# Two-dimensional Fourier mixing and a maxout layer on one core: TensorE's order written out, the input turned on GpSimd

## Chip, cores and metric

The kernel runs on one core of one Trainium2 chip. The metric is device time in microseconds (us) of one execution. Five engines work side by side, each through its own queue in order: TensorE (PE; matmuls, with weight loads shown as PEld), VectorE (DVE), ScalarE (ACT), GpSimd (POOL) and SyncE (SP). Here GpSimd also issues the loads and SyncE the stores.

## The reference

```python
batch, seq, dim = (8, 3072, 256)
def _attn_ref(x):
    X = np.fft.fft(x, axis=1)
    X = np.fft.fft(X, axis=2)
    return X.real.astype(np.float32)

def _moe_ref(x, w1, w2, w3, w_out):          # w1..w3: 256x768, w_out: 768x256
    h = np.maximum(np.maximum(x @ w1, x @ w2), x @ w3)
    return (h @ w_out).astype(np.float32)

def reference(x, moe_w1, moe_w2, moe_w3, moe_w_out):
    a = _attn_ref(x)
    return _moe_ref(a.reshape(8 * 3072, 256), moe_w1, moe_w2, moe_w3, moe_w_out)
```

## The kernel before

**Algebra.** The transform along the sequence is split as 3072 = 24 x 128 into two stages. The transform along the model dimension is folded into the weights: gE, gO and gD are products of the cosine and sine matrices md with the differences w2-w1 and w3-w1; gw and gwr carry w1 and w_out. Because max(a, b, c) = a + max(b - a, c - a, 0), the first layer computes two differences, takes the larger and cuts it at zero; the part of w1 goes straight to the output through gw. The output rows k and 3072-k share their cosine part and differ in the sign of the sine part, so each pair of "plus" and "minus" columns comes out of one accumulation: matmuls with gE and gO give plus, and adding one with gD turns the same accumulator into minus.

**One batch.** `load_x0` (L97) has GpSimd issue 16 DMAs, which cast to bf16 and leave the input as 96 partitions x (128 sequence positions x 64 model columns). `fnet` (L264) does the sequence stages. Stage 1: 64 matmuls of 96 columns (L270), weights x0r[:, :, d], so 128 numbers with a step of 64; groups of five (`DLS`) go to one bank ps1 and are copied to ub by ScalarE (L272). VectorE folds ub into zE and zO (`fold`, L280, and small copies L289 to L297); stage 2 multiplies these with tables cos_t, sin_t, nsin_t (L318 to L326) into ps2, copied to tE and tO by ScalarE (L329); three one-column matmuls make t_mid, the middle row. GpSimd copies tE and tO in reverse to tEr and tOr (L339, L340).

**The layers.** A batch has three blocks of 512 columns and each block six units, one for each 128 columns of the hidden dimension. `unit_plus` (L343) does four 512-column matmuls into two accumulators pse2 and pse3 (L349, L350); `unit_out` (L360) evicts them: ScalarE applies relu to pse2 (L363), VectorE takes the maximum with pse3 (L364) into hp. Later `finish` adds the minus matmuls (L357), and a second `unit_out` writes hm. So a minus matmul waits for the eviction of the plus result. `l2_block` (L376) is a generator of the second layer: four times 16 matmuls of 256 columns (L367, L369, L372) into po, a copy to ot by VectorE (L392), and stores on SyncE's queue. `l2_some(11)` takes eleven of its matmuls after each unit. `l2_mid` (L402) does the middle row of all batches near the end, six rounds of its own.

**What sets the order.** GpSimd's instructions from L133 on stand under `manual_schedule`: they keep the order of the source. TensorE, ScalarE and VectorE are ordered by a planner, which looks for the next ready instruction with estimated times and mostly prefers earlier source. In the source, fnet of batch b+1 stands wholly behind the units of batch b; the planner is free to pull it forward. Buffers: two banks each for ps_f (stages 1 and 2, weight preparation), pse2, pse3 and po; two of x0, tE, tO, tEr, tOr, hp, hm; one of ub, zE and zO.

**The beginning.** Between the first four and the other twelve loads of batch 0, GpSimd makes kidx and dvec (L128, L130); VectorE computes from them the arguments of the tables (L176 to L205), ScalarE the sines. `prep_first` (L220) makes gE, gO, gD after fnet(0); `prep_second` (L240) makes gw and gwr. Loads of the weights (L139, L142) and of batch 1 follow batch 0's on GpSimd's queue.

Of the kernel before, what the change touches and what calls it, by code (L numbers as in the profile page):

```python
# [9 lines left out]
FP32 = mybir.dt.float32  # L10
# [24 lines left out]
def kernel(  # L35
# [48 lines left out]
    v2_bf = consts.tile([128, 2 * DFF], BF16, tag="v2_bf")  # L84
    v3_bf = consts.tile([128, 2 * DFF], BF16, tag="v3_bf")
# [11 lines left out]
    def load_x0(b, between):  # L97
        x0 = x0_pool.tile([96, 128 * 64], BF16, name="x0", tag="x0")
        xr = x[b].rearrange("(a bb) (g dl) -> g a bb dl", bb=128, g=4)
        x0v = x0.rearrange("p (bb dl) -> p bb dl", dl=64)  # L100
        for ch in range(4):
            if ch in between:
                between[ch]()
            for g in range(4):
                nc.gpsimd.dma_start(  # L105
                    out=x0v[g * 24:(g + 1) * 24, ch * 32:(ch + 1) * 32, :],
                    in_=xr[g, :, ch * 32:(ch + 1) * 32, :])
        return x0
# [17 lines left out]
    def between():  # L126

        nc.gpsimd.iota(kidx, [[1, 13], [24, 128]], base=0, channel_multiplier=0,  # L128
                       allow_small_or_imprecise_dtypes=True)
# [3 lines left out]
    with tc.manual_schedule(engines={mybir.EngineType.Pool}):  # L133
        x0_tiles = {0: load_x0(0, {1: between})}

# [8 lines left out]
        x0_tiles[1] = load_x0(1, {})  # L144
# [28 lines left out]
    for (dst, shift) in ((cos_t, 768.0), (sin_t, 0.0)):  # L173
        v = gen.tile([128, 13 * 128], FP32, name="v", tag="v", bufs=2)
        q = gen.tile([128, 13 * 128], FP32, name="q", tag="q", bufs=2)
# [14 lines left out]
    for fc in range(2):  # L190
# [10 lines left out]
        vi = gen.tile([128, 256], INT32, name="vi", tag="vi", bufs=2)  # L201
# [18 lines left out]
    def prep_first():  # L220

        for jh in range(2):
            cs = slice(jh * 384, (jh + 1) * 384)
            for i, (wv, vv) in enumerate(((w2_bf, v2_bf), (w3_bf, v3_bf))):
                w3d, v3d, w13d = (t.rearrange("p (fc j) -> p fc j", fc=2)[:, :, cs]
                                  for t in (wv, vv, w1_bf))
                tc.keep_in_program_order(
                    nc.vector.tensor_tensor(out=v3d, in0=w3d, in1=w13d, op=ALU.subtract))
# [8 lines left out]
                nc.vector.tensor_scalar(out=gD[i][:, cs], in0=gO[i][:, cs], scalar1=dif,  # L237
                                        scalar2=None, op0=ALU.mult)

    def prep_second():  # L240

        for jp in range(NJC // 2):
# [8 lines left out]
            nc.scalar.copy(out=g1t[:, jp * 512:(jp + 1) * 512], in_=pst)  # L251
        psw = ps_f.tile([128, 512], FP32, name="psw", tag="ps")
        for half in range(2):
            for jc in range(NJC):
# [7 lines left out]
                                op0=ALU.mult)  # L262

    def fnet(b, x0):  # L264
        x0r = x0.rearrange("p (bb dl) -> p bb dl", dl=64)
        ub = u_pool.tile([128, 64 * 96], BF16, name="ub", tag="ub")
        for (d0, d1) in DLS:
            ps1 = ps_f.tile([128, 512], FP32, name="ps1", tag="ps")
            for i in range(d1 - d0):
                nc.tensor.matmul(ps1[:, i * 96:(i + 1) * 96], x0r[:, :, d0 + i], m24blk,  # L270
                                 start=True, stop=True)
            nc.scalar.copy(out=ub[:, d0 * 96:d1 * 96], in_=ps1[:, 0:(d1 - d0) * 96])  # L272

# [9 lines left out]
        for ranges in (((20, 45),), ((10, 20), (45, 55)), ((1, 10), (55, 64))):  # L283
            for (dst, op) in ((e, ALU.add), (o, ALU.subtract)):
                for (lo, hi) in ranges:
                    for g in range(2):
                        fold(dst, op, lo, hi, g)
                if ranges[0][0] == 1:
                    nc.vector.tensor_tensor(out=dst[:, 0, 1, 0:24], in0=u[:, 0, 1, :],  # L289
                                            in1=u[:, 0, 3, :], op=op)  # L290
                    if dst is e:
                        nc.vector.tensor_copy(e[:, 0, 0, :], u[:, 0, 0, :])

        nc.vector.tensor_scalar(out=o[:, 0, 0, 1:12], in0=u[:, 0, 2, 13:24], scalar1=-1.0,
                                scalar2=None, op0=ALU.mult)
        nc.vector.tensor_copy(o[:, 0, 0, 13:24], u[:, 0, 2, 1:12])
        nc.vector.tensor_copy(o[:, 0, 0, 24:26], u[:, 0, 2, 0:13:12])  # L297
# [9 lines left out]
        for (tile_i, dst) in ((0, tE), (1, tO)):  # L307
            for g in range(3):
# [20 lines left out]
                nc.scalar.copy(out=dst[:, g * 512:(g + 1) * 512], in_=ps2)  # L329

# [10 lines left out]
        return (tE, tO), (tEr, tOr)  # L341

    def unit_plus(te, to, jc, n):  # L343

        js = slice(jc * 128, (jc + 1) * 128)
        pse2 = ps_l1.tile([128, TOKB], FP32, name="pse2", tag="pse2")
        pse3 = ps_l1.tile([128, TOKB], FP32, name="pse3", tag="pse3")
        for (pse, i) in ((pse2, 0), (pse3, 1)):
            nc.tensor.matmul(pse[:, 0:n], gE[i][:, js], te, start=True, stop=False)  # L349
            nc.tensor.matmul(pse[:, 0:n], gO[i][:, js], to, start=False, stop=True)  # L350
        return pse2, pse3

    def unit_minus(pses, to, jc):

        js = slice(jc * 128, (jc + 1) * 128)
        for i, pse in enumerate(pses):
            nc.tensor.matmul(pse, gD[i][:, js], to, start=False, stop=True,  # L357
                             skip_group_check=True)
# [43 lines left out]
    def l2_mid():  # L402

        hmid = h_pool.tile([128, NJC, B], BF16, name="hmid", tag="hmid")
        for jc in range(NJC):
            pses = unit_plus(t_mid[:, 0, :], t_mid[:, 1, :], jc, B)
            unit_out(pses, hmid[:, jc, :], B)
            yield
        po = ps_o.tile([128, 512], FP32, name="po", tag="po")
        yield from l2_half(po[0:B, 0:256], t_mid[:, 0, :], t_mid[:, 1, :], gw[:, 256:512],  # L410
                           lambda jc: hmid[:, jc, :], B)
        ot = out_pool.tile([128, 512], FP32, name="ot", tag="ot")
        nc.vector.tensor_copy(out=ot[0:B, 0:256], in_=po[0:B, 0:256])
        nc.sync.dma_start(out=out[NHALF: NHALF + S * (B - 1) + 1: S, :], in_=ot[0:B, 0:256])

# [9 lines left out]

    for b in range(B):
        tt = fnet(b, x0_tiles.pop(b))
        if b == 0:
            prep_first()
        tE, tO = tt[0]  # L430
        prev = None

        def finish(prev):
            pses, to, jc, hm = prev
            unit_minus(pses, to, jc)
            unit_out(pses, hm[:, jc, ::-1], TOKB)
# [53 lines left out]
```

## Time and profile before

| what | value |
|---|---|
| median of 3 runs | 500.73 us (500.02 to 501.63) |
| the profiled execution's own time | 499.23 us |
| its span, first to last instruction | 497.1 us |
| mean granted TensorE clock | 0.993 |
| busy: PE, DVE, ACT, POOL | 91%, 64%, 52%, 28% |
| matmuls | 3408 |
| read from HBM, written | 28.31 MB, 25.17 MB |

Profile rows are in microseconds, means in nanoseconds where marked. A busy share is the time in which an engine had an instruction in work; matmuls overlap one another, so the distance between the starts of two matmuls says more than the length of one. In the timeline the columns are start, length, engine, line, operation, output<-inputs and count of merged instructions; in brackets stands the idle time before it and what ended it. In the grouped rows the numbers after the bar are the total busy time, the mean length in nanoseconds, and the idle time before with its cause.

### The profile page before, as it was taken

What the parts mean: (1) busy time and instruction counts of PE and PEld (TensorE: products, weight loads), DVE (VectorE), ACT (ScalarE), POOL (GpSimd) and SP (SyncE); (2) the same over time, 40 slices, a digit from 0 to 9 for tenths busy, and PEclk for the clock granted to TensorE, in tenths of its full rate; (3) what the DMA queues carried; (4) which work ended last, traced back from release to release, by engine and by line L of the source; (5) the groups of instructions that cost most, each with busy time, mean ns of one, the idle gap of its engine ahead of it and who ended that gap; (6) DMA issues with size and microseconds to landing.
All of it is one profiled execution on the core that took longest, in us unless ns stands there. A gap on an engine that the chain in (4) does not pass through costs nothing.

```text
span 497.1 us, 9195 instructions
## 1 busy us (share of the span) xinstructions
PE 453.5 (91%) x3408; PEld 315.6 (63%) x3408; DVE 320.4 (64%) x662; ACT 260.9 (52%) x472; POOL 140.6 (28%) x160
## 2 busy tenths in 40 slices
PE   0056999999999999999999999999999999999995
PEld 0055447785568657785669666875669566866664
DVE  8834674657676576657666567657675666667663
ACT  1355652575436653575446644665457644765440
POOL 9979800029000750029000840048000100020000
PEclk9999899999999999999999999999999999999998
DMA  8999992219921692219911793119911022102122
GB/s 48 75 164 99 98 32 86 84 44 108 105 86 66 59 133 99 73 44 109 126 65 65 74 123 102 65 46 120 134 64 65 22 65 84 65 22 65 65 84 86
DMA packets 163436, 40.05 MB, mean 81 GB/s; under 512 B 136512, under 2 KB 163392, under 8 KB 163392
## 3 DMA queue, kind: packets, MB, share of 16 engines
q0 software_dynamic: 135536, 14.30, 70.6%
q1 hardware_dynamic: 27856, 25.18, 16.1%
q8 instruction: 26, 0.43, 0.4%
q14 instruction: 18, 0.15, 0.1%
HBM read 28.31 MB, written 25.17 MB: 108 GB/s over the span
## 4 chain that ended last, share of the span: by engine, by line
PE 78%; DVE 3%; ACT 2%; POOL 2%; DMA 1%; issue 1%; DVEq 0%; ACTq 0%
PE po L372 23%; PE pse L349 12%; PE pse L357 11%; PE pse L350 11%; PE ps L270 8%; PE po L367 4%; PE po L369 4%; POOL x L105 2%; PE ps L318 2%; DMA x<-in_x_dram 1%; PE ps L324 1%; PE ps L326 1%; ACT stmp L363 1%; PE ps L321 1%; DVE zE L280 1%
## 5 line engine op out<-in xcount | busy, mean ns | idle before, releaser
L363 ACT ACTIVATE stmp<-pse 128x512 bf16<-128x512 f32 (+1 forms) x294 | 167.7, 588 | 164.3 <-PE pse L350 128.6
L364 DVE TENSOR_TENSOR hp<-pse,stmp 128x512 bf16<-128x512 f32 x144 | 99.1, 690 | 99.1 <-PE pse L357 39.8
L105 POOL DMA_DIRECT2D x<-in_x_dram x128 | 109.5, 863 | 8.1 <-DMA x<-in_x_dram 3.6
L349 PE MATMUL pse<-tE,gE 128*128 128x512 bf16 x288 | 108.8, 379 | 1.7 <-DVE hm L364 0.7
L350 PE MATMUL pse<-tO,gO 128*128 128x512 bf16 x288 | 109.1, 380 | 0.0
L364 DVE TENSOR_TENSOR hm<-pse,stmp 128x512 bf16<-128x512 f32 x144 | 99.0, 687 | 11.8 <-ACT stmp L363 9.3
L357 PE MATMUL pse<-tO,gD 128*128 128x512 bf16 x288 | 94.8, 380 | 1.1 <-ACT stmp L363 0.6
L339 POOL COPY tEr<-tE 128x1536 bf16<-128x1536 bf16 x8 | 11.8, 1471 | 289.1 <-ACT tE L329 289.1
L372 PE MATMUL po<-wout_bf,hp 128*128 128x256 bf16 x576 | 92.6, 272 | 0.0
L372 PE MATMUL po<-wout_bf,hm 128*128 128x256 bf16 x576 | 89.1, 272 | 0.1
L270 PE MATMUL ps<-m24blk,x 96*128 96x96 bf16 x512 | 57.4, 250 | 28.8 <-DMA w_bf<-in_moe_w_dram 27.5
L270 PEld LDWEIGHTS <-x 96*128 96x128 bf16 x512 | 55.9, 199 | 33.1 <-DMA w_bf<-in_moe_w_dram 27.4
L392 DVE COPY ot<-po 128x512 f32<-128x512 f32 x96 | 65.5, 684 | 14.5 <-PE po L372 13.8
L372 PEld LDWEIGHTS <-hm 128*128 128x128 bf16 x576 | 56.1, 99 | 17.3 <-DVE hm L364 0.4
L372 PEld LDWEIGHTS <-hp 128*128 128x128 bf16 x576 | 56.2, 100 | 14.2
L272 ACT CAST ub<-ps 128x480 bf16<-128x480 f32 (+1 forms) x104 | 55.4, 554 | 15.6 <-PE ps L270 13.3
L357 PEld LDWEIGHTS <-gD 128*128 128x128 bf16 x288 | 28.1, 98 | 29.8 <-issue 1.5
L350 PEld LDWEIGHTS <-gO 128*128 128x128 bf16 x300 | 29.4, 98 | 27.1 <-issue 12.2
L349 PEld LDWEIGHTS <-gE 128*128 128x128 bf16 x300 | 29.5, 99 | 21.1 <-issue 2.6
L280 DVE TENSOR_TENSOR zE<-ub 128x240 bf16<-128x240 bf16 (+2 forms) x80 | 20.2, 311 | 33.9 <-ACT ub L272 33.9
L367 PE MATMUL po<-gw,tE 128*128 128x256 bf16 x96 | 26.2, 272 | 0.0
L369 PE MATMUL po<-gwr,tOr 128*128 128x256 bf16 x96 | 26.2, 272 | 0.0
(99 smaller groups left out, 359.5 us busy)
## 6 DMA issues: line engine op xcount, KB each, us to landing
out_dram<-ot SPq DMA_DIRECT2D x176, 128.0 KB, 1.7
x<-in_x_dram POOLq DMA_DIRECT2D x128, 96.0 KB, 6.7
out_dram<-ot SPq DMA_DIRECT2D x24, 64.0 KB, 6.7
w_bf<-in_moe_w_dram POOLq DMA_DIRECT2D x6, 192.0 KB, 6.2
out_dram<-ot SPq DMA_DIRECT2D x8, 63.0 KB
wout_bf<-in_moe_w_out_dram POOLq DMA_DIRECT2D x1, 384.0 KB, 8.6
out_dram<-ot SPq DMA_DIRECT2D x1, 8.0 KB
```

The lines of the kernel that those rows point to most:

```text
L105: nc.gpsimd.dma_start(out=x0v[g * 24:(g + 1) * 24, ch * 32:(ch + 1) * 32, :], in_=xr[g, :, ch * 32:(ch + 1) * 32, :])
L270: nc.tensor.matmul(ps1[:, i * 96:(i + 1) * 96], x0r[:, :, d0 + i], m24blk, start=True, stop=True)
L272: nc.scalar.copy(out=ub[:, d0 * 96:d1 * 96], in_=ps1[:, 0:(d1 - d0) * 96])
L349: nc.tensor.matmul(pse[:, 0:n], gE[i][:, js], te, start=True, stop=False)
L350: nc.tensor.matmul(pse[:, 0:n], gO[i][:, js], to, start=False, stop=True)
L357: nc.tensor.matmul(pse, gD[i][:, js], to, start=False, stop=True, skip_group_check=True)
L363: nc.scalar.activation(out=stmp[:, 0:n], in_=pses[0][:, 0:n], func=AX.Relu)
L364: nc.vector.tensor_tensor(out=dst, in0=src3, in1=stmp[:, 0:n], op=ALU.max)
L367: nc.tensor.matmul(po, te, gw[:, 0:256], start=True, stop=False)
L369: nc.tensor.matmul(po, to, wo, start=False, stop=False)
L372: nc.tensor.matmul(po, hcols(jc), wout_bf[:, jc * 256:(jc + 1) * 256], start=False, stop=(jc == NJC - 1))
L392: nc.vector.tensor_copy(out=ot, in_=po)
```

## The change

TensorE and GpSimd both follow the source from the first batch on. The stages of the next batch are a generator of 19 steps (13 stage-1 groups, 6 stage-2 groups), and a table says how many steps run inside each of the 18 units. Folds are issued right after the groups that they need. From batch 1 on, the input lands in four staging tiles xs and GpSimd copies each into x0 in the order of stage 1's weights, so that a weight load reads adjacent numbers; batch 0 keeps the old layout. Minus matmuls of one unit and plus matmuls of the next alternate by accumulator. The middle row is done in two steps of the last batch, from one bank. In the beginning all 16 loads of batch 0 come ahead of kidx and dvec, every second stage-1 group of batch 0 is evicted by VectorE, the four differences of weights are made first and in place, gD is made from PSUM, and prep_second runs as steps of units 1 to 4.

```diff
+    FOLDS = {4: ((20, 45),), 8: ((10, 20), (45, 55)), 12: ((1, 10), (55, 64))}
+    xs_pool = ctx.enter_context(tc.tile_pool(name="xs", bufs=4))
...
+    def fetch_chunk(b, ch):
+        xs = xs_pool.tile([96, 32 * 64], BF16, name="xs", tag="xs")
+        load_chunk(b, ch, xs)
+        return xs
+
+    def turn_chunk(xs, x0, ch):
+
+        nc.gpsimd.tensor_copy(
+            x0.rearrange("p (dl bb) -> p dl bb", bb=128)[:, :, ch * 32:(ch + 1) * 32],
+            xs.rearrange("p (bb dl) -> p dl bb", dl=64))
...
+    with tc.manual_schedule(engines={mybir.EngineType.Pool}):
+        x0_tiles = {0: new_x0(), 1: new_x0()}
+        for ch in range(4):
+            load_chunk(0, ch, x0_tiles[0][:, ch * 2048:(ch + 1) * 2048])
         nc.gpsimd.iota(kidx, [[1, 13], [24, 128]], base=0, channel_multiplier=0,
...
-        x0_tiles[1] = load_x0(1, {})
+        second = [fetch_chunk(1, ch) for ch in range(4)]
...
+        x0r = (x0.rearrange("p (bb dl) -> p dl bb", dl=64) if b == 0 else
+               x0.rearrange("p (dl bb) -> p dl bb", bb=128))
...
+        for i, (d0, d1) in enumerate(DLS):
+            ps1 = ps_f.tile([128, 512], FP32, name="ps1", tag="ps")
+            for k in range(d1 - d0):
+                nc.tensor.matmul(ps1[:, k * 96:(k + 1) * 96], x0r[:, d0 + k, :], m24blk,
+                                 start=True, stop=True)
+            if b == 0 and i % 2:
+                nc.vector.tensor_copy(ub[:, d0 * 96:d1 * 96], ps1[:, 0:(d1 - d0) * 96])
+            else:
+                nc.scalar.copy(out=ub[:, d0 * 96:d1 * 96], in_=ps1[:, 0:(d1 - d0) * 96])
+            if i in FOLDS:
...
+            yield
...
+    def unit_mm(te, to, jc, last):
+
+
         js = slice(jc * 128, (jc + 1) * 128)
...
+        for i in range(2):
+            if last is not None:
+                minus_mm(last, i)
+            pse = ps_l1.tile([128, TOKB], FP32, name=f"pse{i + 2}", tag=f"pse{i + 2}")
+            nc.tensor.matmul(pse, gE[i][:, js], te, start=True, stop=False)
+            nc.tensor.matmul(pse, gO[i][:, js], to, start=False, stop=True)
+            pses.append(pse)
+        return pses
...
+    with tc.manual_schedule(engines={mybir.EngineType.PE, mybir.EngineType.Pool}):
+        tts = {0: []}
+        run(fnet(0, x0_tiles.pop(0), tts[0]), 19)
+        prep_first()
+        for ch in range(4):
+            turn_chunk(second[ch], x0_tiles[1], ch)
...
+                plan = ({6: 2, 7: 2, 8: 2, 9: 2, 10: 2, 11: 2, 12: 1} if b == 0 else
+                        {u: 1 for u in range(13)})
+                plan.update({14: 1, 15: 2, 16: 2, 17: 1})
+            else:
+                steps, plan = mid(), {8: 1, 10: 1}
+            extra = prep_second() if b == 0 else iter(())
+            for u in range(NU):
...
+                pses = unit_mm(tE[:, cs], tO[:, cs], jc, last)
+                if last is not None:
+                    unit_out(last[0], last[3][:, last[2], ::-1], TOKB)
                 unit_out(pses, hp[:, jc, :], TOKB)
...
+                n = 11 if jc < 4 else 10
+                l2_some(n // 2)
+                run(steps, plan.get(u, 0))
+                run(extra, int(1 <= u <= 4))
+                l2_some(n - n // 2)
...
+                if b + 2 < B:
+                    if u == 0:
+                        x0_tiles[b + 2] = new_x0()
+                        fetched = [fetch_chunk(b + 2, 0), fetch_chunk(b + 2, 1)]
+                    if u in (4, 8):
+                        turn_chunk(fetched[u // 4 - 1], x0_tiles[b + 2], u // 4 - 1)
+                        fetched.append(fetch_chunk(b + 2, u // 4 + 1))
+                    if u in (11, 14):
+                        turn_chunk(fetched[u // 4], x0_tiles[b + 2], u // 4)
```

More of the change, by code (lines that the diff above doesn't have):

```diff
@@ L281, in fold @@
                                     in1=u[:, 64 - lo:64 - hi:-1, 3 - g, :], op=op)
[L283 to L292, printed above, removed]
@@ L340, in fnet, with minus_mm @@
         nc.gpsimd.tensor_copy(tOr, tO[:, ::-1])
-        return (tE, tO), (tEr, tOr)
-    def unit_plus(te, to, jc, n):
+        tt += [(tE, tO), (tEr, tOr)]
+        yield
+    def unit_mm(te, to, jc, last):
         js = slice(jc * 128, (jc + 1) * 128)
[L346 to L358, printed above, removed]
+        pses = []
+        for i in range(2):
[6 more added lines that the diff above has]
+        return pses
+    def minus_mm(last, i):
+        pses, to, jc, _ = last
+        nc.tensor.matmul(pses[i], gD[i][:, jc * 128:(jc + 1) * 128], to, start=False,
+                         stop=True, skip_group_check=True)
     def unit_out(pses, dst, n):
```

167 lines of the change are left out of this document (86 added, 81 removed).

## The prediction

> **What bounds the kernel now.** I read the page first: the span, the busy shares, the chain that ended last.
>
> ```profile
> span 497.1 us, 9195 instructions
> PE 453.5 (91%) x3408; PEld 315.6 (63%) x3408; DVE 320.4 (64%) x662; ACT 260.9 (52%) x472; POOL 140.6 (28%) x160
> ...
> PE 78%; DVE 3%; ACT 2%; POOL 2%; DMA 1%; issue 1%; DVEq 0%; ACTq 0%
> ```
>
> TensorE is the bound: 78% of the chain is its own work, and no other engine holds more than 3%. But its 91% counts modelled ends that overlap, so I take its real cost from distances between starts in the timeline (columns: start, length, engine, line, operation).
>
> ```profile
> 109.62 0.38 PE L350 MATMUL pse<-tO,gO 128*128 128x512 bf16 x1
> 109.84 0.38 PE L349 MATMUL pse<-tE,gE 128*128 128x512 bf16 x1
> ...
> 487.98 0.82 PE L372 MATMUL po<-wout_bf,hp 128*128 128x256 bf16 x6
> 488.63 0.27 PE L367 MATMUL po<-gw,tEr 128*128 128x256 bf16 x1
> ...
> 97.20 0.56 PE L270 MATMUL ps<-m24blk,x 96*128 96x96 bf16 x5
> 97.60 0.27 PE L372 MATMUL po<-wout_bf,hp 128*128 128x256 bf16 x1
> ...
> 105.23 0.23 PE L318 MATMUL ps<-cos_t,zE 128*128 128x128 bf16 x1
> 105.30 0.23 PE L321 MATMUL ps<-sin_t,zE 128*128 128x128 bf16 x1
> ...
> 481.10 0.18 PE L349 MATMUL pse<-t_mid,gE 128*128 128x8 bf16 x1
> 481.14 0.17 PE L350 MATMUL pse<-t_mid,gO 128*128 128x8 bf16 x1
> 481.16 0.38 PE L357 MATMUL pse<-tO,gD 128*128 128x512 bf16 x1
> ```
>
> A 512-column matmul costs 0.217 us, a 256-column one 0.65/6 = 0.108, a stage-1 matmul (96 columns, weights read from x with a stride) 0.40/5 = 0.080, a stage-2 one 0.07. One batch holds 108 of 512 columns (23.4 us), 192 of 256 (20.8), 64 of stage 1 (5.1), 50 of stage 2 and three tiny ones (3.7): **53.0 us of dense TensorE work**. What a batch really takes, I read from the once-per-batch reversal on GpSimd:
>
> ```profile
> 164.21 1.47 POOL L339 COPY tEr<-tE 128x1536 bf16<-128x1536 bf16 x1 [38.92 <-ACT tE L329]
> ...
> 439.11 1.47 POOL L339 COPY tEr<-tE 128x1536 bf16<-128x1536 bf16 x1 [50.86 <-ACT tE L329]
> ```
>
> Five batches in 274.9 us: 55.0 each. So the order in which TensorE runs now already hides nearly all: gaps are 2.0 us a batch. Reordering alone can win no more than those, some 14 us over seven batches; the larger sum lies in the 0.080.
>
> The beginning and the end are the rest:
>
> ```profile
> 1.47 3.42 POOL L105 DMA_DIRECT2D x<-in_x_dram  x4 [0.28 <-issue]
> 4.89 1.62 POOL L128 IOTA kidx<- 128x1664 f32 x1
> ...
> 8.88 6.57 POOL L105 DMA_DIRECT2D x<-in_x_dram  x1
> ...
> 9.23 2.07 DVE L176 TENSOR_SCALAR v<-kidx,pidx 128x1664 f32<-128x1664 f32 x2
> ...
> 22.22 0.29 DVE L205 CAST vm<-vi 128x256 f32<-128x256 int32 x1
> ...
> 22.91 0.73 POOL L139 DMA_DIRECT2D w_bf<-in_moe_w_dram  x1
> ...
> 27.46 1.09 PE L270 MATMUL ps<-m24blk,x 96*128 96x96 bf16 x10 [27.46 <-DMA w_bf<-in_moe_w_dram]
> ...
> 37.30 0.33 PE L318 MATMUL ps<-cos_t,zE 128*128 128x128 bf16 x1 [1.66 <-DVE zE L292]
> ...
> 42.59 0.20 PE L334 MATMUL ps<-cos_t,zO 128*128 128x1 bf16 x1
> ...
> 63.69 0.27 PE L367 MATMUL po<-gw,tE 128*128 128x256 bf16 x1
> ...
> 491.45 0.69 DVE L392 COPY ot<-po 128x512 f32<-128x512 f32 x1 [1.05 <-PE po L372]
> ```
>
> GpSimd issues batch 0's 16 loads from 1.47 to 22.91, because one of them stands for 6.57 us while VectorE builds tables; TensorE starts at 27.46 (the DMA named there is a weight's, but x's last load was issued just before it). Stage 2 follows at 37.30, the first second-layer matmul (L367) at 63.69.
>
> **The change part by part.** *Input turned.* From batch 1 on, each of the 64 stage-1 weight loads reads 128 adjacent numbers instead of 128 with a step of 128 bytes. The trace has no such matmul of 96 columns; the bounds are 0.080 (no gain) and 96/512 of 0.217 = 0.041. I take 0.041, because the two 8-column matmuls above, whose weights lie side by side, follow each other within 0.04 and 0.02 us: a packed load is not what holds TensorE. Saving 64 x 0.039 = 2.5 us a batch, seven batches: **-17.5 us**. Batch 0 keeps its stride.
>
> The Trainium skill, "TensorE: Matmul & The Clock Gate", section "Back-to-back issue gap", gives about 81 ns for a sustained pair of weight load and 128-column matmul, which would leave nothing to win here. The 0.07 us of stage 2 is already below it, with strided weights.
>
> *What the turn costs.* Four copies of 96x2048 a batch on GpSimd, absent from the trace. Lower bound: the 1.47 us for 1536 elements, in proportion 2.0. Upper bound from what the same stride does to weight loads:
>
> ```profile
> L270 PEld LDWEIGHTS <-x 96*128 96x128 bf16 x512 | 55.9, 199 | 33.1 <-DMA w_bf<-in_moe_w_dram 27.4
> ...
> L372 PEld LDWEIGHTS <-hm 128*128 128x128 bf16 x576 | 56.1, 99 | 17.3 <-DVE hm L364 0.4
> ```
>
> Twice, hence 3.9. I take 3.0, since the stride is the same but only on the reading side. GpSimd's own sum a batch is 16 loads of 0.86 + 4 x 3.0 + 2 x 1.47 = 29 us of some 52: not a bound. Its queue is in order: reversals of batch b+1, eight loads, a turn (waiting for its chunk to land), four loads, a turn, four loads, two turns. All of it is due a whole batch later, so the turn's own wait hides. Only batch 1's is close (below).
>
> The Trainium skill, "GPSIMD Engine Reference", section "Performance pitfalls for Q7 kernels", puts reads with a step over 8 bytes at half as much again per element; that would be an estimated 2.9 us. No run here has shown it yet.
>
> *The danger in it.* A VectorE operation has stood behind GpSimd's copies:
>
> ```profile
> 44.73 3.21 DVE L237 TENSOR_SCALAR gD<-gO,dif 128x384 bf16<-128x384 bf16 x1 [6.00 <-ACT gO L236]
> ...
> 44.94 1.48 POOL L339 COPY tEr<-tE 128x1536 bf16<-128x1536 bf16 x1
> 46.35 1.47 POOL L340 COPY tOr<-tO 128x1536 bf16<-128x1536 bf16 x1
> ```
>
> It took 3.21 us and ended with the second copy; its fellows take 0.3 to 0.5. The folds (L280, both operands in SBUF) meet no copy before; after, they meet turns. For a fold behind a turn the price lies between 0 and the whole turn. With unit 2.8 us long, chunk 2 lands about 24 us into a batch and its turn runs to 27; the second set of folds becomes ready at about 25. I count one meeting a batch. What does it cost TensorE?
>
> ```profile
> 115.39 0.68 DVE L364 TENSOR_TENSOR hp<-pse,stmp 128x512 bf16<-128x512 f32 x1
> 115.99 0.68 DVE L364 TENSOR_TENSOR hm<-pse,stmp 128x512 bf16<-128x512 f32 x1
> ...
> 157.76 0.87 DVE L280 TENSOR_TENSOR zE<-ub 128x240 bf16<-128x240 bf16 x4 [0.31 <-ACT ub L272]
> 158.55 0.86 DVE L280 TENSOR_TENSOR zO<-ub 128x240 bf16<-128x240 bf16 x4
> ```
>
> Evictions run 0.60 us apart, so a unit keeps VectorE 1.2, plus 12/18 of an output copy (0.4): 1.2 us of 2.8 are free. A set of eight folds takes 1.6, and the minus matmul of the next unit, which waits for the eviction, can bear some 0.5 to 1. So folds alone cost about nothing; folds behind the rest of a turn cost 1 to 2. With 0.5 for all else I take **2 us a batch of stalls**, as many as now: the gaps that the written order closes come back here.
>
> The Trainium skill, "SBUF — State Buffer", section "Who interferes with whom", says that VectorE with two SBUF inputs and a GpSimd instruction reading SBUF exclude each other for a whole instruction. No row before shows it for a fold.
>
> *Order.* TensorE gets steps of one stage-1 group per unit; a step's five matmuls wait for one of two ps banks, emptied by ScalarE in about 0.6 of a 2.8 us unit. Queued behind a late step are the unit's other matmuls and all that follows, nothing overtakes. The tiny middle row goes from six separate rounds at 480 to two steps of batch 7: 24 x 0.03 + 8 x 0.108 = 1.6 us. SyncE's stores are unchanged in number.
>
> *Beginning.* The 16 loads issue without a table beside them: 1.47 + 16 x 0.855 = 15.2, x lands near 20 instead of 27. But kidx now comes behind them, at 16.8 instead of 6.5, and VectorE's tables (9.23 to 22.5: 13.3 us) move to 16.8-30.1. Then 6 copies of ub now on VectorE (at the eviction's 0.6: 3.6) and its folds and small copies (some 5.2): 38.9. So the 7 us won on the load are taken back by VectorE, and **stage 2 starts at 39, where it was 37.3**. Stage 2 as before 5.3 (42.59 - 37.30): 44.4. The weight preparation stands alone on TensorE now, eight groups at about 0.6: 49.2. Six units without second layer, each bound by the eviction chain (two 0.6 on each of ScalarE and VectorE, in turn) at 2.0 to 2.1: **62 us** to the first second-layer matmul, against 63.69. Bounds 57 (ub copies between tables, so stage 1 runs early) and 68 (VectorE behind the four turns of batch 1, or TensorE's first step waiting for them).
>
> *The sum*: 62, then rest of batch 0: 12 units x 1.30 + 128 x 0.108 + 2.6 + 3.7 = 35.8, stalls 2; batches 1 to 6: 6 x (50.5 + 2) = 315.0; batch 7: 23.4 + 20.8 + 1.6 = 45.8; last block: 2 x 0.217 + 64 x 0.108 = 7.3; tail as now 497.1 - 491.45 = 5.7. Together 473.6. Outside the span lie 499.2 - 497.1 = 2.1: 475.7, say **476 us**. The profiled execution, 499.2 in all, stands 0.3% under the median of 500.7.
>
> **The rivals.** *Folds shut out (slower).* VectorE stands behind more than one turn at each of its three sets of folds, as gD did behind two copies. Seven batches hold folds (0 to 6), so it becomes slower than 500.7 when stalls exceed 2 + 24.7/7 = 5.5 us a batch. Three meetings at 3.0 - 0.5 = 2.5 give 7.5, thus 476 + 7 x 5.5 = 514. For: gD's row; against: turns are spread by loads between them, and a fold already running makes GpSimd wait, not VectorE.
>
> *Weights pace unchanged.* Stage 1 stays at 0.080: 476 + 17 = 493. For: no row shows the form. Against: the 8-column rows. The section on the issue gap cited above would have it so.
>
> *Order does not hold.* ScalarE and VectorE are still ordered by the planner; if they run in an order that TensorE's fixed one does not match, each late eviction stops all: 2 more a batch (14) and a beginning at its bound of 68 (6): 496. For: before, TensorE could be placed around folds, and folds had no evictions beside them.
>
> *Nothing meets.* Folds don't wait for turns, beginning at 57: 476 - 7 x 1.2 - 5 = 463.
>
> **How the numbers follow.** Forecast 476: 0.48 (470 to 485). Nothing meets: 0.15. Order does not hold: 0.16. Weights unchanged: 0.07. Folds shut out: 0.14. From 462 to 497 leaves out the slower case and a few mixed ones, some 2 in 10. Within 0.3% (about what a measurement of this kernel tells from no change) 0.04, taken from the two rivals next to it; slower 0.13, faster 0.83.
>
> **What would show it.** Stage-1 starts 0.041 apart in batches 1 to 7; the reversals 52 us apart instead of 55; turns of 2 to 4 us; folds longer than 0.2 to 0.5 where a turn runs; minus matmuls waiting for VectorE there; first load done near 20, stage 2 near 39, first L2 near 62. I am wrong if the fold rows are far over 0.5 in every batch, or if TensorE waits for a turn after batch 1.

## The result, and the profile after

The change made the kernel slower: 559.07 us (median of 4 runs, 558.77 to 563.12) against 500.38 us (4 runs beside them, 499.13 to 501.63). The ratio is 1.119, with a 95% interval of 1.113 to 1.125. The prediction was 476 us, so it was wrong in the sign too. Times are medians of all executions; executions over 1.5% above the fastest of their kernel are left out of the ratios.

The profiled execution took 563.1 us, 561.3 of it span. From the page of the changed kernel: the busy times, the slices of TensorE and of its clock, and the chain:

```profile
PE 433.9 (77%) x3356; PEld 301.3 (54%) x3408; DVE 398.5 (71%) x663; ACT 250.8 (45%) x461; POOL 238.9 (43%) x188
...
PE   0177914995499935999269992999749999999995
...
PEclk9999976998599976999769996899959999999999
...
PE 64%; DVE 24%; issue 6%; POOL 3%; ACT 2%; DMA 0%; DVEq 0%; SPq 0%; POOLq 0%
```

TensorE is busy for less time than before (433.9 us against 453.5), and it has holes: from the sixth slice on, slices with 1 to 5 tenths come back about every five slices, with a lower clock in or behind them. VectorE, 3% of the chain before, holds 24%. Which of its operations grew, the groups by shape tell (total busy time, mean nanoseconds of one):

```profile
L290 DVE TENSOR_TENSOR zO<-ub 128x600 bf16<-128x600 bf16 x16 | 62.3, 3932 | 0.0
L290 DVE TENSOR_TENSOR zE<-ub 128x600 bf16<-128x600 bf16 x16 | 36.3, 2304 | 0.4 <-ACT ub L301 0.4
L290 DVE TENSOR_TENSOR zE<-ub 128x240 bf16<-128x240 bf16 x32 | 6.9, 278 | 3.1 <-ACT ub L301 3.1
```

Of the folds, only those of the first set (600 elements, 25 of the 64 columns) grew, to 2.3 (zE) and 3.9 us (zO) in the mean; undisturbed they take 0.46 (below). The second and third set (240 and 216 elements) kept their 0.27 to 0.28. TensorE's and ScalarE's waits name the operation that is queued behind these folds, the eviction:

```profile
PE pse L384 <- DVE hp L391: 84.1, 7, 18.3
ACT stmp L390 <- DVE hm L391: 83.7, 6, 18.2
```

84 us of TensorE's time went there, in six waits of 10.7 to 18.3 us and a short one. The 32 folds of the first set hold VectorE for 98.6 us where 32 x 0.46 are 14.7: the excess is the same 84 us. One such wait, first VectorE, then GpSimd and TensorE in the timeline of batch 2:

```profile
198.79 6.19 DVE L290 TENSOR_TENSOR zE<-ub 128x600 bf16<-128x600 bf16 x2
204.90 10.27 DVE L290 TENSOR_TENSOR zO<-ub 128x600 bf16<-128x600 bf16 x2
215.09 0.68 DVE L391 TENSOR_TENSOR hm<-pse,stmp 128x512 bf16<-128x512 f32 x1
```

```profile
193.72 3.72 POOL L113 COPY x<-xs 96x2048 bf16<-96x2048 bf16 x1 [0.78 <-PE pse L384]
197.40 3.23 POOL L102 DMA_DIRECT2D xs<-in_x_dram  x4
200.62 3.64 POOL L113 COPY x<-xs 96x2048 bf16<-96x2048 bf16 x1
204.19 3.23 POOL L102 DMA_DIRECT2D xs<-in_x_dram  x4
207.41 7.42 POOL L113 COPY x<-xs 96x2048 bf16<-96x2048 bf16 x2
```

```profile
216.42 0.59 PE L384 MATMUL pse<-tO,gD 128*128 128x512 bf16 x1 [14.55 <-DVE hp L391]
216.79 0.63 PE L377 MATMUL pse<-tE,gE 128*128 128x512 bf16 x1
217.22 0.63 PE L378 MATMUL pse<-tO,gO 128*128 128x512 bf16 x1
```

Four folds, 1.9 us of work, take 16.4 us. The two zE folds are over at 204.98, behind the turn that ends at 204.26; the two zO folds at 215.17, behind the last turn (214.83). The eviction behind them then starts at 215.09, and TensorE, idle for 14.55 us, starts its minus matmul at 216.42. Its 512-column matmuls are then 0.43 us apart, twice the usual. The windows of this wait and of the 5 us behind it (length, busy time of PE, PEld, DVE, ACT and POOL with counts, granted clock) show why:

```profile
201.90:216.40 14.50, 0.00 (x0) 0.00 (x0) 14.50 (x7) 0.54 (x1) 12.83 (x7) 0.59 0.72 43
216.40:221.40 5.00, 4.98 (x22) 2.92 (x22) 1.95 (x3) 1.55 (x4) 0.00 (x0) 0.50 0.20 52
```

For 5 us after the stall the clock is granted at half, which loses 2.5 us more. Per batch, from the reversals:

```profile
182.09 1.46 POOL L363 COPY tEr<-tE 128x1536 bf16<-128x1536 bf16 x1 [35.52 <-ACT tE L351]
250.36 1.46 POOL L363 COPY tEr<-tE 128x1536 bf16<-128x1536 bf16 x1 [35.52 <-ACT tE L351]
...
448.08 1.46 POOL L363 COPY tEr<-tE 128x1536 bf16<-128x1536 bf16 x1 [31.88 <-ACT tE L351]
499.18 1.47 POOL L363 COPY tEr<-tE 128x1536 bf16<-128x1536 bf16 x1 [46.63 <-ACT tE L351]
```

A batch in which folds and turns meet takes 64.6 to 71.6 us (68.3 in batch 2, shown); batch 6, in which nothing is left to turn, takes 51.1. That single batch is what all of them were meant to be.

### The profile page after: what moved, and what is told of

It is laid out like the page before. It is cut to its first block, busy times and chain, and to the rows that moved or that the text cites. A ratio compares the mean times of both kernels' runs of the same rounds, so it can differ in the third digit from the quotient of the medians.

```text
span 561.3 us, 9266 instructions
## 1 busy us (share of the span) xinstructions
PE 433.9 (77%) x3356; PEld 301.3 (54%) x3408; DVE 398.5 (71%) x663; ACT 250.8 (45%) x461; POOL 238.9 (43%) x188
## 4 chain that ended last, share of the span: by engine, by line
PE 64%; DVE 24%; issue 6%; POOL 3%; ACT 2%; DMA 0%; DVEq 0%; SPq 0%; POOLq 0%
PE po L399 19%; DVE zO L290 12%; PE pse L378 11%; PE pse L384 10%; PE pse L377 8%; PE po L394 3%; PE po L396 3%; PE ps L296 3%; DVE zE L290 3%; POOL x L102 2%; DVE hp L391 2%; DVE hm L391 2%; PE ps L340 1%; PE ps L348 1%; PE ps L346 1%
## 5 line engine op out<-in xcount | busy, mean ns | idle before, releaser
L390 ACT ACTIVATE stmp<-pse 128x512 bf16<-128x512 f32 x288 | 158.2, 595 | 154.4 <-DVE hm L391 83.7
L384 PE MATMUL pse<-tO,gD 128*128 128x512 bf16 x288 | 111.8, 389 | 85.9 <-DVE hp L391 84.1
L113 POOL COPY x<-xs 96x2048 bf16<-96x2048 bf16 x28 | 102.8, 3683 | 6.6 <-DMA xs<-in_x_dram 3.9
L301 ACT CAST ub<-ps 128x480 bf16<-128x480 f32 (+1 forms) x98 | 53.6, 554 | 95.1 <-PE ps L296 95.1
L399 PE MATMUL po<-wout_bf,hm 128*128 128x256 bf16 x576 | 94.0, 275 | 0.1
L102 POOL DMA_DIRECT2D xs<-in_x_dram x112 | 91.5, 824 | 3.6 <-DMA xs<-in_x_dram 3.2
L377 PE MATMUL pse<-tE,gE 128*128 128x512 bf16 x238 | 92.2, 387 | 0.0
L290 DVE TENSOR_TENSOR zO<-ub 128x240 bf16<-128x240 bf16 (+2 forms) x80 | 75.7, 1005 | 0.0
L296 PE MATMUL ps<-m24blk,x 96*128 96x96 bf16 x512 | 42.2, 220 | 28.3 <-DMA w_bf<-in_moe_w_dram 20.5
L290 DVE TENSOR_TENSOR zE<-ub 128x240 bf16<-128x240 bf16 (+2 forms) x80 | 49.7, 679 | 6.5 <-ACT ub L301 6.5
L296 PEld LDWEIGHTS <-x 96*128 96x128 bf16 x512 | 36.7, 114 | 31.5 <-DMA w_bf<-in_moe_w_dram 20.4
```

Source lines behind the costliest of these rows:

```text
L102: nc.gpsimd.dma_start(out=dst[g * 24:(g + 1) * 24, :].rearrange("p (bb dl) -> p bb dl", dl=64), in_=xr[g, :, ch * 32:(ch + 1) * 32, :])
L113: nc.gpsimd.tensor_copy(x0.rearrange("p (dl bb) -> p dl bb", bb=128)[:, :, ch * 32:(ch + 1) * 32], xs.rearrange("p (bb dl) -> p dl bb", dl ...
L290: nc.vector.tensor_tensor(out=dst[:, lo:hi, g, 0:24], in0=u[:, lo:hi, g, :], in1=u[:, 64 - lo:64 - hi:-1, 3 - g, :], op=op)
L296: nc.tensor.matmul(ps1[:, k * 96:(k + 1) * 96], x0r[:, d0 + k, :], m24blk, start=True, stop=True)
L377: nc.tensor.matmul(pse, gE[i][:, js], te, start=True, stop=False)
L384: nc.tensor.matmul(pses[i], gD[i][:, jc * 128:(jc + 1) * 128], to, start=False, stop=True, skip_group_check=True)
```

## Experiments

The theory: a fold, which reads both operands from SBUF, can't run beside a GpSimd copy that reads SBUF, and TensorE stands behind the evictions queued after it. Rivals: TensorE's fixed order is at fault, whatever the turns do; or the turns disturb in another way (writes, the extra traffic of GpSimd, late input). Each edit is against the changed kernel if nothing else is said; "before" is run beside it on the same chip.

### Without the turn

```diff
-        second = [fetch_chunk(1, ch) for ch in range(4)]
+        for ch in range(4):
+            load_chunk(1, ch, x0_tiles[1][:, ch * 2048:(ch + 1) * 2048])
...
-        x0r = (x0.rearrange("p (bb dl) -> p dl bb", dl=64) if b == 0 else
-               x0.rearrange("p (dl bb) -> p dl bb", bb=128))
+        x0r = x0.rearrange("p (bb dl) -> p dl bb", dl=64)
...
                     if u in (4, 8):
-                        turn_chunk(fetched[u // 4 - 1], x0_tiles[b + 2], u // 4 - 1)
-                        fetched.append(fetch_chunk(b + 2, u // 4 + 1))
-                    if u in (11, 14):
-                        turn_chunk(fetched[u // 4], x0_tiles[b + 2], u // 4)
+                        ch = u // 4 + 1
+                        load_chunk(b + 2, ch, x0_tiles[b + 2][:, ch * 2048:(ch + 1) * 2048])
```

> The changed kernel without the turn: every batch lands in x0 in the old layout, stage 1 reads its weights with the old stride; order of TensorE, folds, GpSimd's loads and the beginning stay. Theory (a fold with two SBUF operands stands until GpSimd's next turn has ended): no fold of 600 columns over 0.5 us, batch period 51.1 (the undisturbed one at 451 to 502 of the changed kernel) plus 64 x 0.037 = 53.5, total about 485. Rival (the written order and the planner's order of VectorE do not fit, turns or no turns): gaps of 13 us a batch stay, total about 575.

480.37 us, 0.962 of before (0.960 to 0.964). Its groups by shape, and the window of one batch:

```profile
L289 DVE TENSOR_TENSOR zE<-ub 128x600 bf16<-128x600 bf16 x16 | 6.9, 466 | 0.8 <-ACT ub L300 0.6
```

```profile
95.90:149.30 53.40, 53.33 (x419) 38.24 (x418) 35.70 (x74) 30.20 (x56) 15.75 (x18) 1.00 0.75 90
```

The zE folds are at 0.47 us, and TensorE is busy for 53.33 of 53.40 us. So the order holds: the rival that blames it falls, and everything of the change but the turn makes the kernel 18.6 us faster than before (499.0 there).

### A GpSimd instruction that only writes, and one that reads

Against the kernel without the turn: at the turns' places GpSimd writes 3712 numbers into a scratch tile that nobody reads, in one kernel with an iota (3.27 us), in the other with a packed copy from another scratch tile (3.32 us).

```diff
+    def write_only():
+        wr = wr_pool.tile([96, 3712], FP32, name="wr", tag="wr")
+        nc.gpsimd.iota(wr, [[1, 3712]], base=0, channel_multiplier=0,
+                       allow_small_or_imprecise_dtypes=True)
...
                     if u in (4, 8):
+                        write_only()
...
+                    if u in (11, 14):
+                        write_only()
```

> As e1_no_turn, and where the turns stood GpSimd writes 96x3712 numbers into a scratch tile (an iota, about 3.6 us, reads no SBUF). Theory, in the form that the reading of SBUF is what excludes: folds at 0.46, total as e1_no_turn, about 485. Rival (any long GpSimd instruction, or its writing, excludes a fold): folds of 3 to 10 us as with the turn, total about 575.

480.66 us (0.962 of before, 0.960 to 0.965), the folds at 467 and 464 ns: as without it. The two did run at the same time; GpSimd and the first folds of batch 2:

```profile
166.56 3.26 POOL L119 IOTA wr<- 96x3712 f32 x1
...
166.83 0.85 DVE L295 TENSOR_TENSOR zE<-ub 128x600 bf16<-128x600 bf16 x2
```

Then the copy in its place:

```diff
+    src_t = consts.tile([96, 3712], BF16, tag="src_t")
+    nc.vector.memset(src_t, 0.0)
+
     def write_only():
-        wr = wr_pool.tile([96, 3712], FP32, name="wr", tag="wr")
-        nc.gpsimd.iota(wr, [[1, 3712]], base=0, channel_multiplier=0,
-                       allow_small_or_imprecise_dtypes=True)
+        wr = wr_pool.tile([96, 3712], BF16, name="wr", tag="wr")
+        nc.gpsimd.tensor_copy(wr, src_t)
```

> As e3_write_only, but in the turns' places GpSimd copies 96x3712 adjacent bf16 numbers from one scratch tile to another (some 3.6 us, reads SBUF without a stride, result unused). Theory, reading is what excludes: folds of 600 columns of 3 to 10 us again, total 540 to 580. Rival (the stride of the turn or its writing into x0 does it): folds 0.46, total 481.

563.0 us, 1.126 of before (1.123 to 1.129). The groups by shape of the kernel with the copy:

```profile
L122 POOL COPY wr<-src_t 96x3712 bf16<-96x3712 bf16 x28 | 92.9, 3317 | 0.6
L297 DVE TENSOR_TENSOR zE<-ub 128x600 bf16<-128x600 bf16 x16 | 62.6, 3949 | 0.8 <-ACT ub L308 0.6
...
L297 DVE TENSOR_TENSOR zO<-ub 128x600 bf16<-128x600 bf16 x16 | 25.2, 1614 | 0.0
```

Both instructions have the same length, stand in the same places and write a scratch tile (fp32 numbers the iota, bf16 the copy): 82 us lie between the one that reads SBUF and the one that does not. Neither the stride of the turn nor the data it makes is needed for the loss.

### The turn on ScalarE

```diff
-        nc.gpsimd.tensor_copy(
-            x0.rearrange("p (dl bb) -> p dl bb", bb=128)[:, :, ch * 32:(ch + 1) * 32],
-            xs.rearrange("p (bb dl) -> p dl bb", dl=64))
+        for h in range(2):
+            ds = slice(h * 32, (h + 1) * 32)
+            nc.scalar.copy(
+                out=x0.rearrange("p (dl bb) -> p dl bb", bb=128)[:, ds, ch * 32:(ch + 1) * 32],
+                in_=xs.rearrange("p (bb dl) -> p dl bb", dl=64)[:, ds, :])
```

> The turn done by ScalarE in eight pieces of 96x1024 a batch instead of GpSimd in four; all else as changed. Theory: folds at 0.46, batch period 51 to 53 (ScalarE gets some 9 us a batch more and delays a few evictions), total 468 to 485. Rival (any strided reading of xs beside a fold slows it, whoever reads): folds still several us long, total over 520. Rival (order does not fit): over 540.

524.08 us, 1.050 of before (1.046 to 1.055). Its groups by shape:

```profile
L115 ACT COPY x<-xs 96x1024 bf16<-96x1024 bf16 x56 | 107.4, 1975 | 0.0
...
L292 DVE TENSOR_TENSOR zE<-ub 128x600 bf16<-128x600 bf16 x16 | 6.8, 462 | 0.4 <-ACT ub L303 0.4
```

No fold is held, as the theory says. But eight pieces of 1.98 us are 15.8 us a batch on the engine with which each eviction of a unit begins, and the kernel is 44 us slower than the one without the turn, though its weights are adjacent: TensorE waited 23.8 us for ScalarE's relu and 10.8 us for turns. My number missed: I had no row for this copy.

### The turn without the new order

Against the kernel before: loads through staging tiles and turns on GpSimd for batches 2 to 7, with the planner's order as it was, and one buffer less for q to make room.

```diff
+        def turn(xs, ch):
+            nc.gpsimd.tensor_copy(
+                x0.rearrange("p (dl bb) -> p dl bb", bb=128)[:, :, ch * 32:(ch + 1) * 32],
+                xs.rearrange("p (bb dl) -> p dl bb", dl=64))
...
-        q = gen.tile([128, 13 * 128], FP32, name="q", tag="q", bufs=2)
+        q = gen.tile([128, 13 * 128], FP32, name="q", tag="q")
...
-                x0_tiles[b + 2] = load_x0(b + 2, {})
+                x0_tiles[b + 2] = load_turned(b + 2)
```

> The kernel before with one part of the change alone: batches 2 to 7 land in staging tiles and GpSimd turns them; the planner orders TensorE, VectorE and ScalarE as before (one table scratch tile has one buffer instead of two). Theory: the turns run in the first 33 us after the reversals, the folds come some 45 us after them, so they do not meet; six batches gain 2.4 us: 500 - 14 = 486. Rival (the turn itself is what costs, wherever it stands): no gain or slower than before.

507.96 us over six executions (502.38 to 514.71); the ratio is 1.012 (1.007 to 1.017). I expected a gain. The profile is that of the longest execution, so it does not show how the time of the others is made up. Its groups by shape:

```profile
L308 DVE TENSOR_TENSOR zE<-ub 128x600 bf16<-128x600 bf16 x16 | 6.8, 468 | 10.6 <-ACT ub L300 10.6
L288 DVE TENSOR_SCALAR gwr<-gw,sgn 128x256 bf16<-128x256 bf16 x1 | 6.8, 6787 | 0.0
```

The folds don't meet turns here, but the preparation of the weights does: gwr takes 6.8 us instead of the 0.29 that it takes without the turn. It ends with a turn (72.2, the turn at 72.1), TensorE then waits 6.2 us for the eviction behind it, and from the first reversal to the third (44.52 and 174.54 in its timeline) go 130.0 us, where before had 119.3. Later batches take 56.0 us, not the 52.5 that cheaper weights would give; why, I did not find out.

### The turns moved to where no fold is

Here the four turns of batch b+1 stand at the start of batch b, right behind the reversals, on chunks that were fetched a batch earlier; and stage 1 starts at unit 6 in every batch, as batch 0 had it.

```diff
+                x0n = x0_tiles.pop(b + 1) if b == 0 else new_x0()
+                for ch in range(4):
+                    turn_chunk(second[ch], x0n, ch)
+                steps = fnet(b + 1, x0n, tts[b + 1])
+                plan = {6: 2, 7: 2, 8: 2, 9: 2, 10: 2, 11: 2, 12: 1}
...
+                if u == 0 and b + 2 < B:
+                    second = [fetch_chunk(b + 2, ch) for ch in range(4)]
```

> The changed kernel with the same turns at another time: each batch's four turns stand right behind the reversals at its start, from chunks loaded a batch ahead, and the next batch's sixteen loads behind them; all batches run the next batch's stage-1 groups in units 6 to 12, two a unit, as batch 0 does. Theory: turns run some 4 to 19 us after the reversal, folds from 24 us on, none meet; folds 0.46, period 51, total 480.4 - 7 x 2.4 = 464. Rival (a turn costs by itself, wherever it stands, or the order does not bear turns): over 500.

462.39 us, 0.925 of before (0.923 to 0.926): the best of all kernels here, 7.5% under the one before. The same 28 turns run, each 3.75 us. Its timeline on GpSimd and then on VectorE in one batch:

```profile
93.90 1.46 POOL L363 COPY tEr<-tE 128x1536 bf16<-128x1536 bf16 x1 [20.78 <-ACT tE L351]
...
98.31 14.82 POOL L113 COPY x<-xs 96x2048 bf16<-96x2048 bf16 x4
113.06 11.29 POOL L102 DMA_DIRECT2D xs<-in_x_dram  x14
```

```profile
120.25 0.85 DVE L290 TENSOR_TENSOR zE<-ub 128x600 bf16<-128x600 bf16 x2 [0.42 <-ACT ub L301]
121.02 0.85 DVE L290 TENSOR_TENSOR zO<-ub 128x600 bf16<-128x600 bf16 x2
```

The turns are over at 113, the folds come at 120, beside the issue of loads with no turn behind them, and take 0.46 each again; so the issue of loads by itself does not hold a fold. A batch takes 50.75 us. The edit also moves stage 1 to fewer units, so it is not the turns' place alone; but with the folds at 0.46 in both, the 18.0 us against the kernel without the turn are 2.6 us a batch, what the adjacent weights were to bring.

### The folds moved behind the turns

First only by the table, so that the first set comes with the last steps of stage 1:

```diff
-    FOLDS = {4: ((20, 45),), 8: ((10, 20), (45, 55)), 12: ((1, 10), (55, 64))}
+    FOLDS = {11: ((20, 45),), 12: ((10, 20), (45, 55), (1, 10), (55, 64))}
```

> The changed kernel with one line changed: the first set of folds is issued behind stage-1 group 11 instead of 4, the other two behind group 12; turns stay where they are. Theory: from batch 1 on the turns have ended some 33 us after the reversal and the folds begin at 36, so folds 0.46 and periods of 51 to 54 (twelve folds in a row delay an eviction); in batch 0 turns of 68 to 89 still meet folds at about 80, once 5 to 15 us. Total 470 to 485. Rival (the turn costs wherever it stands): about 560 as changed.

542.66 us, against the 470 to 485 expected; the executions lie between 527.7 and 547.9, so no ratio is given. The edit didn't do what it was for: in batch 1 the folds still started 16.7 us behind the reversal (128.37 against 111.67), because VectorE is ordered by the planner, which pulled them forward. They lasted 2.1 and 2.7 us in the mean. So VectorE was made to follow the source as well:

```diff
+    with tc.manual_schedule(engines={mybir.EngineType.PE, mybir.EngineType.Pool,
+                                     mybir.EngineType.DVE}):
```

> As e7_fold_late, and VectorE too keeps the order of the source from batch 0's units on, so that the planner can no longer pull the first folds forward (in e7 they still came 16.7 us after the reversal). Turns stay where the change put them. Theory: folds begin at some 36 us after the reversal, behind the last turn at 33: 600-column folds 0.46 from batch 1 on, periods 51 to 54, one meeting in batch 0; total 465 to 485. Rival (a turn costs wherever the folds are, for instance through other VectorE work): periods near 61 as in e7.

494.05 us, 0.989 of before (0.986 to 0.993), so 65 us less than with the change, still 32 more than with the turns moved, and above the 465 to 485 expected. Its timeline on VectorE in batch 3, the wait of TensorE there, and the windows of batches 1 and 3:

```profile
249.45 1.15 DVE L290 TENSOR_TENSOR zE<-ub 128x600 bf16<-128x600 bf16 x2
...
253.08 1.57 DVE L290 TENSOR_TENSOR zE<-ub 128x240 bf16<-128x240 bf16 x8
```

```profile
257.86 0.38 PE L384 MATMUL pse<-tO,gD 128*128 128x512 bf16 x1 [2.17 <-DVE hp L391]
```

```profile
106.10:158.60 52.50, 50.65 (x419) 35.54 (x418) 35.42 (x74) 30.27 (x56) 30.65 (x22) 1.00 0.72 91
...
214.70:269.10 54.40, 52.23 (x419) 36.37 (x418) 35.66 (x74) 30.36 (x56) 30.66 (x22) 0.97 0.73 88
```

In batch 3 the folds run nearly at their normal length, but the 16 smaller ones and the copies now stand together ahead of an eviction, and TensorE waits 2.2 us for it; with the slower clock behind the wait the batch takes 54.4 us. In batch 0 folds still met turns (TensorE waited 9.6 us there), and in batches 2 and 5 the first fold did, for 2.4 and 1.5 us. In batch 1 no fold met a turn: TensorE waited 1.85 us for the bunch, the clock stayed at 1.00, and the batch took 52.5 us. So two prices are told apart: folds in one bunch cost 1.4 us a batch (52.5 against the 51.1 of batch 6 in the changed kernel), 3.3 where the clock fell behind the wait, held ones 14 to 20.

### One copy in a batch

Against the kernel without the turn: one packed copy of 3.3 us in each of batches 0 to 5, behind all loads, and 2 us of a write-only instruction, in a first kernel ahead of the loads and in a second between them and the copy. The diff leads from the first to the second:

```diff
                 if u == 0 and b + 2 < B:
                     x0_tiles[b + 2] = new_x0()
-                    write_only()
                     for ch in range(4):
                         load_chunk(b + 2, ch, x0_tiles[b + 2][:, ch * 2048:(ch + 1) * 2048])
+                    write_only()
                     read_copy()
```

> The kernel without the turn (480.4 us, folds of 464 ns, a batch every 53.35 us), with one packed copy of 96x3712 on GpSimd (3.3 us) in each of batches 0 to 5, behind 2 us of a write-only instruction and sixteen loads. The first folds of a batch start at +17.6 after the reversal, the copy runs from about +19.3 to +22.6; so they start while loads are issued and no copy runs. If a fold is held by a copy that stands next in the queue, the first fold lasts about 5.3 us, its batch loses 4 to 6 us, and the total is about 500 to 512. If only a copy that runs holds a fold, the first three pass at 0.46, at most the last waits for 3.3, and the total is 481 to 492. If one meeting costs 1 to 2 us, as the prediction had it, 486 to 490.

481.15 us, 0.962 of before (0.958 to 0.966), all folds at 466 and 463 ns. It missed its aim in part: the loads waited for their queue now and then, so the copies ran later than planned (from 117.07 in batch 1, 21.3 us behind the reversal). The last fold of a set started 1.4 us or more ahead of the copy. The time is that expected if only a running copy holds a fold, but since no fold came near a copy, it does not tell the two cases apart.

> The same, with the write-only instruction of 2 us moved between the loads and the copy: the first folds start at +17.6 while it runs (+17.3 to +19.3). If a copy that stands next holds folds whatever runs ahead of it, the first fold again lasts about 5.3 us and the total is that of the kernel with the loads ahead, 500 to 512. If the issue of loads is needed for it, the folds pass at 0.46 until the copy starts, at most the last one is held, and the total is 481 to 492.

493.35 us, 0.987 of before (0.982 to 0.992). In the profiled execution, 489.3 us, one fold of all was held by the copy, in batch 1. GpSimd, VectorE (the last two folds of the set) and TensorE there, and the windows of this batch and the next:

```profile
117.89 2.06 POOL L126 IOTA wi<- 96x2270 f32 x1
119.87 3.29 POOL L122 COPY wr<-src_t 96x3712 bf16<-96x3712 bf16 x1
```

```profile
118.89 0.46 DVE L302 TENSOR_TENSOR zO<-ub 128x600 bf16<-128x600 bf16 x1
...
119.27 4.23 DVE L302 TENSOR_TENSOR zO<-ub 128x600 bf16<-128x600 bf16 x1
```

```profile
124.75 0.38 PE L396 MATMUL pse<-tO,gD 128*128 128x512 bf16 x1 [3.26 <-DVE hp L403]
```

```profile
100.58:158.77 58.19, 54.48 (x412) 38.91 (x418) 39.34 (x74) 30.29 (x56) 21.04 (x21) 0.97 0.79 83
158.77:212.06 53.29, 52.91 (x412) 38.18 (x418) 35.66 (x74) 30.18 (x56) 21.16 (x21) 1.00 0.76 90
```

This is the price of one meeting by itself: the fold is 3.8 us longer, TensorE waits 3.26 us, runs the next 5 us at a granted clock of 0.66, and the batch takes 58.2 instead of 53.3, 4.9 us more. The held fold started 0.6 us before the copy did and ended 0.34 us after it; the one before, started 1.0 us ahead of the copy, passed, as did others 0.8 us ahead in batches 2 and 5. In batch 0 the same copy held another operation, the scaling gwr (59.12 to 64.24; 0.29 us long without a copy), and that batch lost about as much (58.0 us, against 53.4 with the copy behind the loads).

## Where the prediction was right, and where it failed

**The failed step** is "2 us a batch of stalls", made of "I count one meeting a batch" at the price of "folds behind the rest of a turn cost 1 to 2". Measured are 14 to 20 us: the batches with turns took 64.6 to 71.6 us, those without held folds 51.1 (here) and 50.75 (turns moved; 51.3 in batch 0). Six batches lost 84 us of waiting and some 15 us at half clock; the sum without its stalls, 462, and these 99 us make 561, and 559 were measured. (The prediction counts seven batches with a meeting; batch 6 has nothing to turn, so there are six.) What happened is the rival "Folds shut out", whose mechanism the experiments show, but whose size (514 us) I also had too small. Three things in that step were off.

- *The price of one meeting.* I let VectorE's slack and the half to one microsecond that the minus matmul can bear absorb most of it. By itself one meeting cost 4.9 us: TensorE waited for nearly the whole delay of the fold, 3.3 of 3.8 us, and then ran for 5 us at 0.66 of its clock.
- *Where they meet.* I put chunk 2's turn at 24 to 27 us into a batch, against the second set of folds, and priced no other pair in the sum. That turn came about there, but in batch 2 the four turns started 11.6, 18.5, 25.3 and 29.0 us behind the reversal, the last two back to back, and the first set of folds came at 16.7, in their midst. The second set came behind the stall and met none.
- *How long one meeting lasts.* I took the rest of a running turn. Folds also waited while loads were issued between two turns, and to the end of the turn behind them; the four folds of a set met up to four turns one after the other. The rival had three meetings at 2.5 us.

I argued against the rival that loads between the turns spread them. They did not help: a gap of four loads is 3.2 us, and a fold that started 0.7 us into it (204.90, where the loads began at 204.19) was held through the loads and the turn behind them. Nor did GpSimd wait for folds instead, the other argument: no turn took longer than 3.93 us.

**Right:** the price of the weights. Stage 1 of the changed kernel, from the timeline:

```profile
222.83 0.38 PE L296 MATMUL ps<-m24blk,x 96*128 96x96 bf16 x5
223.05 0.27 PE L394 MATMUL po<-gw,tE 128*128 128x256 bf16 x1
```

Five matmuls in 0.22 us are 0.043 each, against 0.041 predicted and 0.080 before; the rival "Weights pace unchanged" falls. The 81 ns in the section "Back-to-back issue gap" of the Trainium skill's "TensorE: Matmul & The Clock Gate" are for 128 columns; they are no bound for the 96-column matmuls here, at 43 ns.

**Right:** the beginning. Stage 1, stage 2 and the first second-layer matmul started at

```profile
20.46 1.10 PE L296 MATMUL ps<-m24blk,x 96*128 96x96 bf16 x10 [20.46 <-DMA w_bf<-in_moe_w_dram]
...
37.47 0.33 PE L340 MATMUL ps<-cos_t,zE 128*128 128x128 bf16 x1 [1.66 <-DVE zE L290]
...
61.78 0.27 PE L394 MATMUL po<-gw,tE 128*128 128x256 bf16 x1
```

where 20, 39 and 62 were predicted.

**Mis-sized without effect:** the turn, 3.68 us (3.0 taken, bounds 2.0 to 3.9):

```profile
L113 POOL COPY x<-xs 96x2048 bf16<-96x2048 bf16 x28 | 102.8, 3683 | 6.6 <-DMA xs<-in_x_dram 3.9
```

The estimate of 2.9 us from the Trainium skill, "GPSIMD Engine Reference", section "Performance pitfalls for Q7 kernels", is as far off: per element the turn costs 1.80 ns, the packed copy above 3317/3712 = 0.89, so twice and not half as much again.

**Wrong, in the other direction:** that the written order wins nothing of its own, since stalls would come back. Without the turn the batches took 53.4 us against 55.0, with TensorE busy throughout, and from the first to the last reversal (42.33 to 416.05) 373.7 us against 394.2 before; nearly half of that, 9.4 us, fell in batch 0 (53.6 against 62.9). Without its seven times 2 us of stalls the sum would have been 462, and the kernel with moved turns took 462.4. That the rival "Nothing meets" (463) gives about the same is in part luck: it took 5 us from a shorter beginning, which did not come (62.1 to the first second-layer matmul there).

**Falls:** "Order does not hold"; the kernel without the turn has the same order and no hole.

The Trainium skill says in "SBUF — State Buffer", section "Who interferes with whom", that a VectorE instruction with two inputs in SBUF contends with a GpSimd instruction that reads SBUF, and not with one that only writes it. The two runs with the iota and the packed copy agree: 480.7 and 563.0 us. I had named this rule and the row of gD, and then priced it as one chance meeting. A resource that excludes for whole instructions, on an engine whose queue feeds the bound, had to be placed in time, operation by operation; the table of folds and the queue of GpSimd gave all that was needed for it.

## What to carry to other kernels

A copy on an idle engine is free only if nothing on the way to the bound shares a resource with it: look which operations such copies hold (here those with two operands in SBUF, and a scaling), and when they run, and put GpSimd's reading copies where none of these run. The same 28 turns cost about 100 us between the folds and about nothing ahead of them. An engine's work under a written order still runs as early as its inputs allow; where a place in time matters, it has to be enforced by data, or by what stands ahead of it in the queue.

## What the runs showed of the hardware

- A fold can be held before the copy starts. In batch 2 the first fold started at 198.79, 1.4 us after the last turn had ended and 1.8 before the next, and the pair ended at 204.98. Behind a write-only instruction a fold 0.6 us ahead of the copy was held and one 1.0 us ahead passed. The Trainium skill, "SBUF — State Buffer", section "Who interferes with whom", lets the later one to issue wait until the earlier has finished; here no copy was in work when the fold began. The guess that the next copy takes the resource while it still stands in GpSimd's queue fits, but it is not shown, and what sets its reach is not settled: in batch 2 a fold 2.5 us ahead of the next turn was held (204.90, the turn at 207.41), while behind sixteen loads folds 1.4 us or more ahead of a single copy passed.
- The hold isn't confined to two SBUF operands: gwr, one tensor operand and a column of scalars, took 5.1 and 6.8 us where a copy ran beside it, and 0.29 without.
- After a stall of 14.55 us TensorE's clock was granted at 0.50 for 5 us. After shorter waits the length alone does not tell: with VectorE kept in order, 5 us at 0.66 followed waits of 2.0 to 2.6 us in batches 2 to 5, while 1.00 followed 1.85 us in batch 1 and 2.66 us in batch 0.
- ScalarE copied 96x1024 bf16 with a step of 128 bytes in 1.98 us; GpSimd needs 3.7 us for twice as many.
